# A long-convolution block and a linear-attention block in one kernel: the first inverse DFT stage in 32-row array tiles, with new channel groups, shift weights spread by a matmul, a shorter index computation and a new order

## The chip, the cores and the metric

The kernel runs on one core of a Trainium2 chip. The metric is the device time in microseconds of one execution; the median of three runs is given. Profile times are counted from the first instruction of the program. Engines are named as in the profile: PE is TensorE's matmuls and PEld its weight loads, DVE is VectorE, ACT is ScalarE, POOL is GpSimd, and SP is SyncE, which issues all DMAs here.

## The reference

Two independent blocks on 2048 positions and 576 channels, in bf16, side by side in the output:

```python
# A: gated long convolution
k_shift = sum over t < 4 of shift_k[:, t] * (k delayed by t)
kv = k_shift * v
y = irfft(rfft(pad(kv, 2S)) * rfft(pad(ssm_k, 2S)))[:S]     # along the 2048 positions, per channel
a = q * (y + kv * ssm_D)
# B: linear attention, 32 heads of 18 channels
q, k, v = split(x @ wqkv);  phi(t) = where(t > 0, t + 1, exp(t)) + 1e-6
kv = phi(k)^T v ;  z = sum phi(k)                            # per head
b = (phi(q) kv / (phi(q) z + 1e-6)) @ wo
out = concat(a, b)
```

## The kernel before

Block A does the transforms as matmuls. A position is split as 16 a + b with 128 values of a and 16 of b. The 576 channels come in five chunks (`ACH`, ci = 0 to 4), four of 128 and one of 64. For every chunk the same stages run on `ssm_k` (key h) and on the product kv (key u):

- `hl`, `hT`: load the rows of ssm_k and transpose them on PE (16 transposes of 128 x 128).
- `cv` (four stages): k_shift times v, on DVE or POOL, in place over v.
- `h1`, `u1` (`s1`, L460): first stage, for each b a matmul of 128 rows with the table `G[ri]` (ri = 0 cosine, 1 sine); 8 values of b make a unit, copied out of PSUM to `Ch` or `Cu`.
- `ht`, `ut` (`tr`, L467): a DMA transpose SBUF to SBUF, half a chunk (hf = 0, 1) at a time.
- `h2`, `u2` (`s2`, L483): second stage, the 16-point part: eight matmuls of 64 rows by 32 columns with 512 moving columns, into `T` (for h) or `SU` (for u).
- `pX`, `pT`: the products of the two spectra, on DVE.
- `i1` (L507): first inverse stage, below.
- `i2` (L520, L521): second inverse stage, with `F[ri]`, the transposed tables (`FT`), then the multiplication by q on DVE; `st` stores.

A half of `T` or `X` holds, on the 128 partitions, four bands of 32: (r, j), with r the pair and j the member. Before, an i1 unit treats one z of one half. For each of four column groups it accumulates four matmuls of 64 rows (a pair of bands) and 128 moving columns of the 16-point table `K.W`, for both pairs r; the two pairs lie in different row tiles of the array and write different PSUM banks. One unit is 32 matmuls, one PSUM tile and one copy to `V`. `K.W` has 128 columns, three quarters of which a mask makes zero in every row.

Block B has units `k` (L397) and `q` (L406), the projections from `xT` with phi on ACT (exp) and DVE (L389, L390); `G` (L570), phi(k)^T x; `kv`, `M`, `den`, `bc`; and `o` (L644), the output projection, whose result ACT copies to `ob` and SP stores. `xd` loads x transposed by DMA, `xl` loads it plain, `lw` loads the weights of q (0) and k (1).

All PSUM tiles come from one pool of four buffers of two banks each. The inputs k, v and q come in three channel groups (`GRP`) of 256, 256 and 64 channels (`kl`, `vl`, `ql`); v and q of the first two groups share two buffers.

Before the stages, a setup makes the tables. DVE multiplies two iotas into the index `mp` (L138), takes it modulo 8192 (L139), makes `ident` (L62), and makes `mc`, the index moved by three quarters of a turn, in two steps (L142, L143). ACT takes the sine of `mp` (`sin.1`) and of `mc` (`sin.0`), L212. Of the 16-point tables, index and mask are made on POOL and DVE (`iw`, `wk`, `iv`, `sw`, `W`). `wu.40` is 40 matmuls on zeros. The shift weights are loaded with a DMA that writes them to all 128 partitions (`ls`, `Wall`), and ACT reorders them to `Wj`.

What runs when is written by hand in `ORDER`: a list of units such as `i1.0.0.1.A` (chunk 0, half 0, z 1, copied by ACT). Each unit issues its instructions on every engine's queue in that order, and each engine works through its queue in order. A letter A, D or P at the end chooses the engine.

Of the kernel before, what the change touches and what calls it, by code (L numbers as in the profile page):

```python
# [26 lines left out]
ACH = [(0, 128), (128, 128), (256, 128), (384, 128), (512, 64)]  # L27
# [3 lines left out]
wm io wu.0 ix.0 sin.1 id ix.1 hl.0 iw wk wu.40 sin.0 hT.0.D FT.1.D h1.0.0.0.A h1.0.1.0.A FT.0.D h1.0.1.1.A  # L31
h1.0.0.1.A iv sw W lw.0 xd.2 q.2.0 hc lw.1 k.8 q.2.2 q.2.1 ls Wj hl.1 hT.1.D k.9 k.11 k.10 h1.1.1.0.D xd.0 k.3
kl.0 cv.0.0.D one h1.1.0.0.A k.1 ht.0.0 h2.0.0.0.A h2.0.0.1.A eps cv.0.1.DD cv.0.2.DD q.0.1 h1.1.1.1.A q.0.0
h1.1.0.1.A xd.3 q.3.0 q.0.2 vl.0 cv.0.3.PDD k.2 cv.1.0.P k.0 ht.0.1 h2.0.1.1.A q.3.1 k.12 u1.0.1.1.A k.15
h2.0.1.0.D ht.1.1 h2.1.1.0.A k.13 u1.0.0.1.A hl.2 hT.2.D u1.0.0.0.A cv.1.1.PD k.14 xd.1 u1.0.1.0.A xl.2
cv.1.2.DD cv.1.3.DPP ht.1.0 xl.1 h2.1.1.1.A q.1.1 h2.1.0.1.A h2.1.0.0.A q.1.0 q.1.2 h1.2.1.0.A ut.0.1 k.7
u2.0.1.0.D u2.0.1.1.A k.6 h1.2.0.1.A k.4 ut.0.0 u2.0.0.1.D u2.0.0.0.A k.5 pX.0.0 pT.0.0 u1.1.1.0.A u1.1.1.1.A
q.3.2 u1.1.0.1.A xl.0 xl.3 kl.1 pX.0.1 pT.0.1 u1.1.0.0.A es G.0 vl.1 h1.2.0.0.A h1.2.1.1.A cv.2.0.D cv.2.1.DD
cv.2.2.DD G.2 ut.1.0 G.4 u2.1.0.1.D u2.1.0.0.A ut.1.1 i1.0.0.1.A hl.3 i1.0.0.0.A i1.0.1.1.A i1.0.1.0.A
cv.2.3.DDD ql.0 cv.3.0.D cv.3.1.DD u2.1.1.1.A ht.2.0 u2.1.1.0.A pX.1.1 pT.1.1 hT.3.A G.1 lwv pX.1.0 pT.1.0  # L40
h2.2.0.1.A ht.2.1 G.3 cv.3.2.DD u1.2.0.0.A i2.0.0 kl.2 u1.2.1.1.A u1.2.1.0.A kv u1.2.0.1.A i2.0.1 h2.2.0.0.A
h2.2.1.0.A den h2.2.1.1.A i1.1.1.0.A lwo M.0 i1.1.0.1.A i1.1.0.0.A i1.1.1.1.D ut.2.0 u2.2.0.0.A M.2 ut.2.1
bc.3.0 u2.2.0.1.A bc.0.1 h1.3.0.1.A bc.4.0 h1.3.0.0.A bc.0.0 h1.3.1.1.A vl.2 h1.3.1.0.A hl.4 ht.3.0 i2.1.1 M.1
# [68 lines left out]
def _small(tc, cpool, slot, K):  # L112
# [9 lines left out]
    nc.vector.memset(K.negpi[:], -math.pi)  # L122
    K.warm = cpool.tile([128, 1], FP32, name="warm")
# [7 lines left out]
def _dft_index(tc, slot, K, part):  # L131

    nc = tc.nc
    if part == 0:
        kap = K.sm[:, 128:256].unsqueeze(1).to_broadcast([128, 16, 128])
        sv = K.sm[:, 256:272].unsqueeze(2).to_broadcast([128, 16, 128])
        K.mp = slot([128, 16, 128], I32, "mp")
        nc.vector.tensor_tensor(out=K.mp[:], in0=kap, in1=sv, op=ALU.mult)  # L138
        nc.vector.tensor_single_scalar(out=K.mp[:], in_=K.mp[:], scalar=8191, op=ALU.bitwise_and)  # L139
    else:  # L140
        K.mc = slot([128, 2, 16, 128], I16, "mc")
        nc.vector.tensor_single_scalar(out=K.mc[:, 0], in_=K.mp[:], scalar=6144, op=ALU.add)  # L142
        nc.vector.tensor_single_scalar(out=K.mc[:, 1], in_=K.mc[:, 0], scalar=8191, op=ALU.bitwise_and)  # L143


def _w16_index(tc, K):
# [21 lines left out]
    iota(sm[:, 384:448], [[1, 16], [0, 4]])  # L168
    for c, shift, mask in ((6, 1, 127), (8, 0, 1)):
# [23 lines left out]
def _w16_mask(tc, K):  # L193
# [5 lines left out]
    K.wz = K.sm[:, 1152:1536]  # L199
    nc.gpsimd.memset(K.wz, 1.0 / S)  # L200
    for p in (0, 64):
        m = K.wz[p:p + 64].rearrange("p (y z) -> p y z", z=4)
        nc.gpsimd.affine_select(out=m, in_=m, compare_op=ALU.is_ge, fill=0.0, base=0, pattern=[[0, 96], [-16, 4]],
                                channel_multiplier=1)
        nc.gpsimd.affine_select(out=m, in_=m, compare_op=ALU.is_ge, fill=0.0, base=15, pattern=[[0, 96], [16, 4]],
                                channel_multiplier=-1)


def _sine(tc, cpool, K, ri):
    K.G[ri] = cpool.tile([128, 16, 128], BF, name="G%d" % ri)  # L210
    src = K.mp[:] if ri else K.mc[:, 1]
    tc.nc.scalar.activation(out=K.G[ri][:], in_=src, func=ACT.Sin, scale=TWO_PI / 8192, bias=K.negpi[:])  # L212
# [512 lines left out]
```

## Time and profile before

| | |
|---|---|
| median of 3 runs | 171.53 us (171.33 to 173.3) |
| profiled execution, device time | 171.81 us |
| its span, first to last instruction | 170.0 us |
| PE busy | 159.0 us (94%) |
| DVE, ACT, POOL busy | 139.7, 122.8, 70.9 us (82%, 72%, 42%) |
| DMA, mean over the span | 192 GB/s, 32.58 MB |

The profile's page gives the busy time of each engine and then the span in 40 slices of 4.25 us, where a digit is the busy share in tenths. The groups collect equal instructions: count, busy time, mean duration, then the engine's idle time before them and what ended it. Matmuls overlap, so their mean duration is a latency and not a pitch. The chain of waits is followed back from the last instruction: each piece gives start, duration, engine, output and line, and how many instructions it merges. The timeline gives start, time to the end of the last one, engine, line, operation and shapes.

### The profile page before, as it was taken

Reading aid. Unit: us, or ns where it says so; the run is one execution under the profiler, and the core shown is the slowest. Engines: PE = TensorE matmul, PEld = TensorE weight load, DVE = VectorE, ACT = ScalarE, POOL = GpSimd, SP = SyncE. Lnnn points to the kernel's source line nnn. Section 1 sums busy time; section 2 is a strip of 40 time slices with the busy share of each in tenths; the row PEclk is TensorE's granted clock in tenths of the full one; section 3 lists DMA queues with packets and bytes.
Section 4 is the critical chain, followed back from the end, with each engine's and each line's share of the span. In section 5 each row is a group of like instructions: output and inputs, shape, how many; then the busy total and the mean of one; then the engine's idle time right before and its main releaser. Section 6 shows DMA issues by size and latency. Waiting matters only on the chain.

```text
span 170.0 us, 4984 instructions
## 1 busy us (share of the span) xinstructions
PE 159.0 (94%) x2176; PEld 106.9 (63%) x2176; DVE 139.7 (82%) x159; ACT 122.8 (72%) x142; POOL 70.9 (42%) x76
## 2 busy tenths in 40 slices
PE   4779999999999799999999999999999999999990
PEld 4768566665575456565685586857856765677750
DVE  7995589998989867999599887997999777999530
ACT  3458987977788899923597477989897778784431
POOL 7998982027693397000000049999900400000000
PEclk9999999999999999999999999999999999999997
DMA  5999699799989999999998655980959957988685
GB/s 147 273 268 250 119 267 136 137 272 225 145 183 217 263 178 318 290 213 219 306 214 196 106 150 40 182 159 18 146 126 276 202 128 69 237 180 258 191 244 117
DMA packets 81704, 32.58 MB, mean 192 GB/s; under 512 B 57432, under 2 KB 80978, under 8 KB 81682
## 3 DMA queue, kind: packets, MB, share of 16 engines
q1 hardware_dynamic: 81682, 32.26, 91.0%
q8 instruction: 17, 0.28, 0.7%
q14 instruction: 5, 0.04, 0.1%
HBM read 15.48 MB, written 4.72 MB: 119 GB/s over the span
## 4 chain that ended last, share of the span: by engine, by line
PE 77%; DMA 11%; DVE 6%; ACT 3%; issue 0%; ACTq 0%
PE q_ps L406 12%; PE g_ps L570 12%; PE k_ps L397 11%; PE o_ps L644 10%; PE s_ps L460 8%; PE i_ps L507 8%; DMA Ctu<-Cu 7%; PE s_ps L483 5%; DMA Cth<-Ch 4%; PE hT_ps L443 2%; PE i_ps L520 2%; PE i_ps L521 2%; PE bc_ps L635 1%; PE kv_ps L583 1%; DVE mp L138 1%; DVE mp L139 1%
## 5 line engine op out<-in xcount | busy, mean ns | idle before, releaser
L429 POOL TENSOR_TENSOR at<-k,Wj 128x2048 bf16<-128x2048 bf16 (+1 forms) x5 | 16.4, 3289 | 36.3 <-DVE at L430 36.2
L406 PE MATMUL q_ps<-xT,wqk 128*126 128x512 bf16 (+1 forms) x100 | 23.3, 381 | 0.0
L644 PE MATMUL o_ps<-wo_M,pqT 126*128 126x512 bf16 (+3 forms) x160 | 21.9, 286 | 0.0
L397 PE MATMUL k_ps<-wqk,xT 128*128 128x512 bf16 (+1 forms) x160 | 21.8, 286 | 0.0
L460 PEld LDWEIGHTS <-G 128*128 128x128 bf16 x320 | 17.6, 98 | 5.2 <-issue 2.1
L570 PE MATMUL g_ps<-pk,x_sb 128*128 128x512 bf16 (+3 forms) x160 | 20.4, 286 | 0.0
L277 ACT ACTIVATE Cu<-s_ps 128x1024 bf16<-128x1024 f32 (+1 forms) x18 | 16.6, 951 | 2.8 <-PE s_ps L460 2.4
L397 PEld LDWEIGHTS <-xT 128*128 128x128 bf16 x160 | 11.4, 98 | 11.1 <-issue 1.1
L644 PEld LDWEIGHTS <-pqT 126*128 126x128 bf16 (+1 forms) x160 | 11.2, 97 | 10.7 <-issue 0.8
L406 PEld LDWEIGHTS <-wqk 128*126 128x126 bf16 (+1 forms) x100 | 12.5, 131 | 8.2 <-issue 1.2
L277 ACT ACTIVATE Ch<-s_ps 128x1024 bf16<-128x1024 f32 (+1 forms) x18 | 16.3, 952 | 1.4 <-PE s_ps L460 0.8
L507 PE MATMUL i_ps<-W,T 64*128 64x128 bf16 x288 | 16.6, 216 | 0.4 <-DVE pqT L638 0.4
L649 ACT ACTIVATE ob<-o_ps 128x576 bf16<-128x576 f32 x16 | 10.4, 653 | 8.9 <-PE o_ps L644 8.7
L570 PEld LDWEIGHTS <-x_sb 128*128 128x128 bf16 (+1 forms) x160 | 10.8, 101 | 9.5 <-issue 0.2
L507 PE MATMUL i_ps<-W,X 64*128 64x128 bf16 x288 | 16.5, 216 | 0.0
L277 ACT ACTIVATE T<-s_ps 128x1024 bf16<-128x1024 f32 x16 | 15.8, 1021 | 0.6 <-PE s_ps L483 0.6
L277 ACT ACTIVATE V<-i_ps 128x1024 bf16<-128x1024 f32 x14 | 13.6, 1027 | 2.8 <-PE i_ps L507 2.1
L390 DVE SCALAR_TENSOR_TENSOR pqT<-pqT,q_ps 126x1024 bf16<-126x1024 bf16 (+1 forms) x12 | 12.2, 1037 | 3.8 <-ACT pqT L389 3.8
L522 DVE TENSOR_TENSOR q<-i_ps,q 128x1024 bf16<-128x1024 f32 (+1 forms) x10 | 11.2, 1116 | 4.6 <-PE i_ps L521 4.6
L389 ACT ACTIVATE pqT<-q_ps,neg 126x1024 bf16<-126x1024 f32 (+1 forms) x12 | 11.6, 968 | 4.3 <-PE q_ps L406 4.3
L430 POOL TENSOR_TENSOR at<-at 128x2048 bf16<-128x2048 bf16 (+1 forms) x4 | 12.4, 3094 | 5.4 <-DVE at L429 5.2
L433 POOL TENSOR_TENSOR v<-at,v 128x2048 bf16<-128x2048 bf16 (+1 forms) x3 | 10.3, 3419 | 9.8 <-DVE at L430 9.6
(120 smaller groups left out, 335.4 us busy)
## 6 DMA issues: line engine op xcount, KB each, us to landing
x_sb<-in_B_x_dram SPq DMA_DIRECT2D x4, 576.0 KB
out_dram<-ob SPq DMA_DIRECT2D x16, 144.0 KB, 4.0
h_sb<-in_A_ssm_k_dram SPq DMA_DIRECT2D x4, 512.0 KB
k<-in_A_k_dram SPq DMA_DIRECT2D x2, 1024.0 KB, 9.1
v<-in_A_v_dram SPq DMA_DIRECT2D x2, 1024.0 KB, 6.6
q<-in_A_q_dram SPq DMA_DIRECT2D x2, 1024.0 KB
out_dram<-q SPq DMA_DIRECT2D x2, 1024.0 KB
wqk<-in_B_wqkv_dram SPq DMA_DIRECT2D x2, 576.0 KB
```

The source lines that it names most:

```text
L277: nc.scalar.activation(out=out, in_=in_, func=ACT.Copy)
L389: nc.scalar.activation(out=out_ap, in_=ps_ap, func=ACT.Exp, bias=K.neg1[0:n, :])
L390: nc.vector.scalar_tensor_tensor(out=out_ap, in0=out_ap, scalar=1.0, in1=ps_ap, op0=ALU.min, op1=ALU.max)
L397: nc.tensor.matmul(ps[:, n0:n1], lhsT=xT[r // 4][:, t, rr * 128:(rr + 1) * 128], rhs=wqk[:, t, D + n0:D + n1], start=(t == 0), stop=(t == 4))
L406: nc.tensor.matmul(ps[0:hn, j, :], lhsT=wqk[:, t, h0:h0 + hn], rhs=xT[g][:, t, :], start=(t == 0), stop=(t == 4))
L429: on[0].tensor_tensor(out=t_, in0=kk[:, 3 - stage:19 - stage], in1=wb(stage), op=ALU.mult)
L430: on[1].tensor_tensor(out=a_, in0=a_, in1=t_, op=ALU.add)
L460: nc.tensor.matmul(ps[:, bi, 0:dc], lhsT=K.G[ri][:, b, :], rhs=xf(b), start=True, stop=True)
L507: nc.tensor.matmul(ps[:, r, g, :], lhsT=s[key, hf][64 * r:64 * r + 64, z, x, 128 * g:128 * g + 128], rhs=K.W[64 * r:64 * r + 64, m, :], st ...
L522: nc.vector.tensor_tensor(out=qs, in0=ps[:, :, 0:dc], in1=qs, op=ALU.mult)
L570: nc.tensor.matmul(ps[0:fn, n0:n1], lhsT=x_sb[:, r, f0:f0 + fn], rhs=pk[:, r, n0:n1], start=(r == 0), stop=(r == 15))
L644: nc.tensor.matmul(ps[:, n0:n1], lhsT=pqT[0:hn, c, r * 128:(r + 1) * 128], rhs=B['M'][0:hn, c, n0:n1], start=(c == 0), stop=(c == 4))
```

## The change

- The first inverse stage treats a whole half per unit, in bands of 32 rows: 128 matmuls of 32 rows and 64 moving columns, with the four bands (r, j) next to each other in program order, each in its own row tile of the array and its own PSUM bank. A unit holds two PSUM tiles and makes two copies. `K.W` shrinks to 64 columns, half of them zero in every row; its mask is made with one comparison on DVE instead of four POOL instructions; the factor 1/S moves from it to the copies of `FT`.
- So that the bands come out in that arrangement, `s1` reads its moving operand in a new channel order (runs of 8 channels), `s2` reads `Ct` in a contiguous order, and `i1` copies to `V` in runs of two.
- k, v, q come in two groups of 320 and 256 channels; the chunk of 64 channels is now the third of five. Each group of v and q has a buffer of its own (v's, then q's). `st` stores in three parts, the second group in two halves.
- The shift weights are loaded to one partition and spread over 128 by a matmul with a row of ones (`Wj.0`, `Wj.1`, `Wj.2`: 512 + 512, 512 + 512 and 256 columns), and copied by ACT to `Wj`.
- The index is reduced with a pair of shifts to the range -4096 to 4095, and `mc` is its absolute value (one instruction); the cosine is taken with a bias of half pi.
- `ORDER` is another one throughout. On DVE the two memsets of `wqk` (`wm`) stand behind the `FT` copies, and the memset of `ones1` behind the setup's index operations.

Two functions that transpose x on PE are defined and used by no unit of the order (left out below).

```diff
-ACH = [(0, 128), (128, 128), (256, 128), (384, 128), (512, 64)]
+ACH = [(0, 128), (128, 128), (256, 64), (320, 128), (448, 128)]
 ORDER = """
-wm io wu.0 ix.0 sin.1 id ix.1 hl.0 iw wk wu.40 sin.0 hT.0.D FT.1.D h1.0.0.0.A h1.0.1.0.A FT.0.D h1.0.1.1.A
-h1.0.0.1.A iv sw W lw.0 xd.2 q.2.0 hc lw.1 k.8 q.2.2 q.2.1 ls Wj hl.1 hT.1.D k.9 k.11 k.10 h1.1.1.0.D xd.0 k.3
...
+io hl.0 wk hl.1 wu.0 wu.40 ix.0 id sin.1 ix.1 iw ls Wj.2.A sin.0 lw.1 hT.0.D Wj.0.A Wj.1.A FT.1.D FT.0.D wm
+h1.0.1.1.A h1.0.0.0.A h1.0.0.1.D iv h1.0.1.0.A hT.1.D xd.1 sw k.5 one W k.4 k.6 lw.0 q.1.1 q.1.2 q.1.0 hc xd.3
...
+u1.3.1.1.A u1.3.1.0.D M.1 den h2.3.0.1.A ht.3.1 cv.4.1.PP cv.4.2.PP h2.3.0.0.A i1.2.0.AA hT.4.D M.2 h2.3.1.1.A
+i2.2.1 h2.3.1.0.A i2.2.0 h1.4.0.1.A bc.2.1 ut.3.0 M.0 h1.4.0.0.A bc.2.0 u2.3.0.1.A bc.3.1 ut.3.1 h1.4.1.1.A
+bc.4.1 pX.1.1 h1.4.1.0.A pT.1.1 M.4 u2.3.0.0.A ht.4.0 i1.1.0.AA bc.1.1 u2.3.1.1.A bc.0.1 M.3 bc.0.0 u2.3.1.0.A
+ht.4.1 i1.1.1.AA bc.3.0 cv.4.3.PPD o.8 pX.3.1 h2.4.0.1.A h2.4.0.0.A bc.4.0 o.15 u1.4.0.1.A bc.1.0 u1.4.1.1.A
...
+o.5 u2.4.1.0.A u2.4.1.1.D pX.4.1 pT.4.1 ql.1 o.7 o.0 u2.4.0.0.A i1.3.0.DA o.2 o.1 u2.4.0.1.D pX.4.0 pT.4.0 st.0
+i1.4.1.AD o.4 o.10 i1.4.0.AD i2.3.0 o.6 i2.4.0 st.1 i2.4.1 i2.3.1 o.14 st.2 o.3 o.12 o.11
 """
...
 def _dft_index(tc, slot, K, part):
-        nc.vector.tensor_single_scalar(out=K.mp[:], in_=K.mp[:], scalar=8191, op=ALU.bitwise_and)
+        nc.vector.tensor_scalar(out=K.mp[:], in0=K.mp[:], scalar1=19, scalar2=19, op0=ALU.logical_shift_left,
+                                op1=ALU.arith_shift_right)
     else:
-        K.mc = slot([128, 2, 16, 128], I16, "mc")
-        nc.vector.tensor_single_scalar(out=K.mc[:, 0], in_=K.mp[:], scalar=6144, op=ALU.add)
-        nc.vector.tensor_single_scalar(out=K.mc[:, 1], in_=K.mc[:, 0], scalar=8191, op=ALU.bitwise_and)
+        K.mc = slot([128, 16, 128], I16, "mc")
+        nc.vector.scalar_tensor_tensor(out=K.mc[:], in0=K.mp[:], scalar=-1.0, in1=K.mp[:], op0=ALU.mult, op1=ALU.max)
...
 def _w16(tc, cpool, K):
-    K.W = cpool.tile([128, 3, 128], BF, name="W16")
-    nc.vector.tensor_tensor(out=K.W[:].rearrange("p m n -> p (m n)"), in0=K.wz, in1=ws[:, 64:448], op=ALU.mult)
+    K.W = cpool.tile([128, 3, 64], BF, name="W16")
+    nc.vector.scalar_tensor_tensor(out=K.W[:].rearrange("p m n -> p (m n)"), in0=K.wz, scalar=K.tb, in1=ws[:, 64:256],
+                                   op0=ALU.is_equal, op1=ALU.mult)
...
-    Wall = slotv([128, D, 4], BF, "Wall")
+    Wrow = slotv([1, D, 4], BF, "Wrow", 1)
+    ones1 = lpool.tile([1, 128], BF, name="ones1")
...
     def load_shift():
-        nc.sync.dma_start(out=Wall[:].rearrange("p d j -> p (d j)"),
-                            in_=A_shift_k.rearrange("d j -> (d j)").partition_broadcast(128))
-    def shift_w():
-        nc.scalar.activation(out=Wj[:], in_=Wall[:].rearrange("p d j -> p j d"), func=ACT.Copy)
+        nc.vector.memset(ones1[:], 1.0)
+        nc.sync.dma_start(out=Wrow[:].rearrange("p d j -> p (d j)"), in_=A_shift_k.rearrange("(o d) j -> o (d j)", o=1))
+    def shift_w(i, eng='A'):
+        d0, dn = ((0, 256), (256, 256), (512, 64))[i]
+        ps = psum.tile([128, 256, 4], FP32, name="w_ps", tag="big")
+        for d in range(0, dn, 128):
+            n = min(128, dn - d)
+            nc.tensor.matmul(ps[:, d:d + n, :], lhsT=ones1[:], rhs=Wrow[:, d0 + d:d0 + d + n, :], start=True, stop=True)
+        evict(Wj[:, :, d0:d0 + dn], ps[:, 0:dn, :].rearrange("p d j -> p j d"), eng)
...
-    GRP = ((0, 256), (256, 256), (512, 64))
+    GRP = ((0, 320), (320, 256))
...
     def s1(ci, xf, key, bg, ri, eng='A'):
-            nc.tensor.matmul(ps[:, bi, 0:dc], lhsT=K.G[ri][:, b, :], rhs=xf(b), start=True, stop=True)
+            nc.tensor.matmul(ps[:, bi, 0:dc].rearrange("p (z h y) -> p z h y", z=2, y=8), lhsT=K.G[ri][:, b, :],
+                             rhs=xf(b).rearrange("p (h z y) -> p z h y", z=2, y=8), start=True, stop=True)
...
-    def i1(ci, hf, z, eng='A'):
+    def i1(ci, hf, eng='AA'):
...
-        ps = psum.tile([128, 2, 4, 128], FP32, name="i1_ps", tag="big")
-        for g in range(4):
-            for n, (key, x, m) in enumerate((('T', 0, 0), ('T', 1, 1), ('X', 0, 2), ('X', 1, 2))):
-                for r in range(2):
-                    nc.tensor.matmul(ps[:, r, g, :], lhsT=s[key, hf][64 * r:64 * r + 64, z, x, 128 * g:128 * g + 128],
-                                     rhs=K.W[64 * r:64 * r + 64, m, :], start=(n == 0), stop=(n == 3))
-        d = dc // 2 * z + 32 * hf
-        evict(V[:, :, d:d + 32].rearrange("p j (g t) -> p g j t", t=4),
-              ps[:].rearrange("p r g (j t) -> p (r g) j t", t=4), eng)
+        ps = [psum.tile([128, 2, 2, 4, 64], FP32, name="i1_ps", tag="big") for _ in range(2)]
+        for z in range(2):
+            for g in range(4):
+                for n, (key, x, m) in enumerate((('T', 0, 0), ('T', 1, 1), ('X', 0, 2), ('X', 1, 2))):
+                    for r in range(2):
+                        for j in range(2):
+                            q = 32 * (2 * r + j)
+                            nc.tensor.matmul(ps[r][:, j, z, g, :], lhsT=s[key, hf][q:q + 32, z, x, 128 * g:128 * g + 128],
+                                             rhs=K.W[q:q + 32, m, :], start=(n == 0), stop=(n == 3))
+        for r in range(2):
+            d = 64 * hf + 32 * r
+            evict(V[:, :, d:d + 32].rearrange("p j (c t) -> p c j t", t=2),
+                  ps[r][:].rearrange("p j z g (n t) -> p (j z g) n t", t=2), eng[r])
...
 def f_T(ri, eng='D'):
-        evict(K.F[ri][:], ps[:], eng)
+            nc.vector.tensor_single_scalar(out=K.F[ri][:], in_=ps[:], scalar=1.0 / S, op=ALU.mult)
```

More of the change, by code (lines that the diff above doesn't have):

```diff
@@ L39 @@
[L39 to L43, printed above, removed]
@@ L122, in _small @@
     nc.vector.memset(K.negpi[:], -math.pi)
+    K.halfpi = cpool.tile([128, 1], FP32, name="halfpi")
+    nc.vector.memset(K.halfpi[:], math.pi / 2)
     K.warm = cpool.tile([128, 1], FP32, name="warm")
@@ L167, in _w16_index @@
     iota(sm[:, 32:64], [[0, 2], [1, 16]])
-    iota(sm[:, 384:448], [[1, 16], [0, 4]])
-    for c, shift, mask in ((6, 1, 127), (8, 0, 1)):
+    iota(sm[:, 384:416], [[1, 16], [0, 2]])
+    for c, shift, mask in ((6, 1, 127), (8, 0, 1), (10, 0, 16)):
         n = sm[:, c:c + 1].bitcast(I32)
```

87 lines of the change are left out of this document (47 added, 40 removed).

## The prediction, made before the changed kernel was run

> **What bounds the kernel now.** I read the page first: busy shares, then the slices.
>
> ```profile
> span 170.0 us, 4984 instructions
> PE 159.0 (94%) x2176; PEld 106.9 (63%) x2176; DVE 139.7 (82%) x159; ACT 122.8 (72%) x142; POOL 70.9 (42%) x76
> PE   4779999999999799999999999999999999999990
> ```
>
> TensorE (PE) has work in every slice but the first three, one of 7 and the last. So a microsecond of PE work taken out of the middle is worth about a microsecond, as long as DVE, at 82%, doesn't become the bound. Second, the groups with shapes kept apart, and the chain of waits in order of time:
>
> ```profile
> L507 PE MATMUL i_ps<-W,T 64*128 64x128 bf16 x288 | 16.6, 216 | 0.4 <-DVE pqT L638 0.4
> L397 PE MATMUL k_ps<-wqk,xT 128*128 128x64 bf16 x80 | 4.9, 193 | 0.0
> ```
>
> ```profile
> 18.82 3.24 PE q_ps L406 x15
> ...
> 61.87 0.56 PE s_ps L483 x16
> 62.43 1.33 PE k_ps L397 x10
> 63.76 0.45 PE s_ps L460 x8
> 64.20 1.23 PE k_ps L397 x10
> ...
> 105.38 0.11 PE den_ps L614 x19
> ...
> 148.01 3.72 PE i_ps L507 x128
> ```
>
> The means in the groups are latencies of overlapping matmuls; the chain gives the pitch. 15 matmuls of 512 columns take 3.24 us, 216 ns each. A k block is five of those and five of 64 columns: 1.23 - 5 x 0.216 = 0.15 us, so a matmul of 64 columns with its own load of 128 weights takes 30 ns. Four i1 units (L507, 128 matmuls of 64 rows, two row tiles at once) take 3.72 us: 0.93 us a unit, 58 ns a pair. The k block right after an s2 stretch, whose matmuls sit in 64 x 32 tiles, takes 1.33 instead of 1.23 us: changing the array's tiling costs 0.10 us. And 19 matmuls of one column in four column tiles take 0.11 us, 5.8 ns each: where four tiles lie side by side, load and matmul can issue that fast.
>
> Third, the start, in PE's timeline and in the chain:
>
> ```profile
> 2.40 4.45 PE L73 MATMUL warm_ps<-sm 128*128 128x128 bf16 x40 [2.40 <-DVE sm L75]
> 7.84 1.86 PE L443 MATMUL hT_ps<-ident,h_sb 128*128 128x128 bf16 x16 [1.00 <-DVE ident L62]
> 9.50 1.90 PE L529 MATMUL ft_ps<-ident,G 128*128 128x128 bf16 x16
> 12.56 1.07 PE L460 MATMUL s_ps<-hT,G 128*128 128x128 bf16 x16 [1.16 <-ACT G L212]
> 13.46 1.06 PE L529 MATMUL ft_ps<-ident,G 128*128 128x128 bf16 x16
> ```
>
> ```profile
> 2.34 2.16 DVE mp L138
> 4.52 2.13 DVE mp L139
> 6.65 1.14 DVE ident L62
> 7.79 1.08 DVE mc L142
> 8.89 1.59 DVE mc L143
> ```
>
> Until about 12 us a DVE chain sets the time, and PE runs at half rate: the first 16 transposes take 9.50 - 7.84 = 1.66 us (104 ns each), the FT of 13.46 only 0.90 (56 ns).
>
> **First inverse stage.** Before: 18 units x 0.93 = 16.7 us. After: nine units of 128 matmuls, each 32 rows by 64 columns, in four row tiles, so 32 groups of four. No row shows four row tiles with 64 columns. Lower bound of a group: 27 ns, half of a pair's 58 less some fixed part; the nearest rows are the 64-column matmul with its load (30 ns) and the four column tiles (4 x 5.8 = 23 ns), so I take 30. Upper bound: 4 x 29 = 116 ns, if row tiles do not overlap beyond the rate at which the pairs issue today. At 30 ns a unit is 0.96 us, nine are 8.6: **-8.1 us**, all on PE in the second half, where PE sets the time.
>
> **Changes of tiling.** Counting in the two orders the places where an i1, s2 or den unit stands beside another kind gives 49 before and 62 after, since each i1 now stands alone: 13 x 0.10 = **+1.2 us**.
>
> **The start.** The two memsets of wqk (0.99 to 2.19 on DVE) go behind the FTs, so mp starts at about 1.3, when POOL's iotas (0.91 and 1.11, up to 0.24 us long) are done. Then 2.25 (2.27 to 4.52 today) + 2.13 (shift pair, priced as L139) + 1.14 (ident) = 6.8. One step makes mc out of two int32 operands: between 1.59 (L143) and 2.25 (L138), nearer the second: 9.05. That is 1.4 us earlier than today. But the first Wj matmul has been put ahead of hT on PE, and it waits for the ones1 memset, which stands on DVE behind mc and six small index operations (four take 0.4 us today): 9.7. Behind that matmul on PE stands hT, which could have run at 6.9; behind its copy on ACT stands the cosine (sin.0), which then ends at 12.8 instead of 12.5. So PE: hT at 9.95 instead of 7.84, at half rate to 11.6; four Wj matmuls of 512 columns at half rate, 4 x 0.43, to 13.3; then FT.1. Today the rate doubled after 3.4 to 4.7 us of steady work (7.84 to between 11.20 and 12.56); from 9.75 that is 13.1 to 14.5. With 14.5, FT.1 ends at 14.8, FT.0 at 15.7, the four first s1 at 17.5. Today these are done at 15.27: **+2.2 us**. With 13.1 it is +1.4; if the rate rises only behind FT.0 (the 40 warm-ups ran 4.45 us without it), +3.1.
>
> [...]
>
> **Loads.** hl.1 goes ahead of the first x (0.52 MB more before it; at the 1.0 MB in 6.6 us of a v load, +3.4 us). Today's x is in by 14.6, as its POOL memset runs there without a wait; the first k unit now asks at about 18.5, so hidden, with half a microsecond left. The 0.59 MB broadcast of the shift weights goes, which pays for k's first group being 320 channels wide; the first conv today runs at 30.0 without a wait. ql.1 (1.05 MB) now stands in the tail, behind three output stores on SP. From there to i2.3.0, which needs it, lie six o units (7.4), three i1 (2.9), two s2 (0.5) and an i2 half (0.9), 11.7 us, against 6.6 to 9.1 to land: 0, and if that cover were gone, its lateness moves the end one to one.
>
> **Costed at nothing.** s1 reads its moving operand in runs of 8 elements; no row shows that. Nearest is the strided stationary operand of hT, 62 against 56 ns: 0 to 6 ns x 320 = 0 to +2.0 us; I take 0, as a run of 8 lies nearer to contiguous than hT's single elements. A gain below today's 56 ns is excluded by the 128 columns. FT's copy now multiplies: 0 to +0.9 (L139 for the same size). V's copies write runs of 2 instead of 4: today runs of 4 cost 1027 against 1022 ns contiguous, so 0; the 18 copies stay 18. Conv on POOL grows by two full operations; POOL is at 42%.
>
> **Waits.** PE waits for buffers and transposes after the start add up to some 3.4 us today. An i1 now needs two of the four PSUM tiles at once, and its two copies (ACT, 0.94 each) last longer than its matmuls. I added PE, ACT and DVE by stretches of 15 us of PE work, each unit at its row: behind the start, DVE or ACT exceed PE by 1.7 us before and 4.2 after, worst around M.1 to o.8 (PE 17.3, DVE 19.6, ACT 19.9). So -3.4 (all waits gone) to +2.5; I take 0, because units may slide across a stretch's edge and the order is a new one throughout.
>
> **Sum.** 170.0 - 8.1 + 1.2 + 2.2 + 0 = 165.3 us of span. The profiled execution took 171.81, 1.8 outside its span: 167.1. The median of the runs, 171.53, lies 0.3 below that execution: **166.8 us**.
>
> **Rivals.**
> *Waits take it back*: the two-tile i1 and a busier DVE cost +2.5 to +4 in the middle: 169.3 to 170.8. For: DVE would be at about 137 of 165. Against: today's order holds PE waits to 3.4 us at 82%.
> *The row tiles issue one after the other*: in the first inverse stage each of 1152 matmuls takes the 29 ns that one of a pair takes today: 33.4 us, +16.7 instead of -8.1: 191.6 us, slower. Break-even is a group of four at 46 ns. For: no row has four row tiles, and a pair never runs under 58 ns. Against: the 5.8 ns of the four column tiles, and 58 ns is just the time of 128 columns.
> [...]
> *Only two of four run at once* (the change doesn't do what it says): 60 ns a group, 17.3 us, +0.6 instead of -8.1: 175.5.
> *Runs of 8 halve s1's rate*: 256 x 56 + 64 x 30 ns = +16.3: 183. Against: hT's far worse stride costs 10%.
>
> **How the numbers follow.** Forecast 0.61, its own range 163.4 (all waits gone) to 168.9 (start +3.1, runs +1.2). Waits take it back 0.21; only two at once 0.07; one after the other 0.06; halved s1 0.05. A difference of 2% (168.1 to 175.0) is about what a measurement of this kernel tells from no change. Faster: 0.57 of the forecast and 0.05 of the waits, 0.62; the rest of these two and half of "two at once" is within 2%, 0.22; slower 0.16. The range for 8 in 10 takes in forecast and waits: 162.5 (a bit below "all waits gone", for groups at 27 ns) to 172.5.
>
> **What would show it.** Right: 128 i1 matmuls in about 0.96 us; the first s1 ending near 17.5 with hT behind a Wj matmul; s1 still 0.45 us per 8; ACT and DVE waits of PE around M.1 to o.8. Wrong: an i1 unit over 1.5 us, s1 over 0.55 us per 8, i2.3.0 waiting for q, or PE gaps of over 6 us behind the start.

## The result, and the profile after

The changed kernel takes 194.91 us (median of 4 runs, 194.64 to 197.28) against 172.18 for the kernel before on the same chip: 1.135 times as long, 95% interval 1.123 to 1.146. The prediction was 166.8 us, in a range of 162.5 to 172.5, so it was wrong by 28 us and in its sign. Ratios in this document leave disturbed runs out; a median does not, so where the two differ the ratio is the figure to read.

The page of the changed kernel, the same rows as those shown of before, with the granted clock:

```profile
span 192.6 us, 6147 instructions
PE 164.9 (86%) x2757; PEld 105.6 (55%) x2757; DVE 147.6 (77%) x161; ACT 124.9 (65%) x146; POOL 71.1 (37%) x70
PE   7399999999999999859999914869779949987692
PEclk9859999999999999966999985999999996999999
```

Every engine's share fell: nothing became a bound by its amount of work. PE now has holes in the middle (the 1 near 113 us, the 4 behind it) and in the last third, and behind them the granted clock drops to 0.50. Measuring how far each matmul's start lies behind the median pace of its kind (line, tile and shape), PE loses 22 to 27 us more behind 20 us than before; the figure depends on the excess from which one counts. That is most of the 27 us between the predicted span (165.3) and the measured one.

Two things that the sum counted on did come. The start, in the chain of waits (start, duration, what):

```profile
3.62 1.23 DVE mp L141
4.85 0.23 DVE ident L61
...
8.21 0.38 PE w_ps L365
8.59 1.86 PE hT_ps L464 x16
...
15.52 1.92 PE s_ps L481 x32
```

The first four s1 are done at 17.44; 17.5 was predicted. And the row tiles run four at once, as PE's timeline shows of one i1 unit (8 matmuls to a row, start and latency):

```profile
154.96 0.25 PE L532 MATMUL i_ps<-W,T 32*128 32x64 bf16 x8
155.03 0.20 PE L532 MATMUL i_ps<-W,X 32*128 32x64 bf16 x2
157.89 0.23 PE L532 MATMUL i_ps<-W,X 32*128 32x64 bf16 x6 [2.66 <-issue]
158.06 2.14 PE L673 MATMUL o_ps<-wo_M,pqT 126*128 126x512 bf16 x8
```

In the undisturbed stretches of these units eight matmuls start every 62 to 65 ns, 31 to 33 ns to a group of four; 30 was predicted. But two matmuls into the second row's eight, PE stands still for 2.86 us. "issue" means that the profile shows nothing that it waited for: no operand, no buffer, no semaphore. The o unit behind it runs at half rate for a while (eight matmuls in 2.14 us, with a granted clock of 0.50 from 158.44 us; at the end of the kernel forty take 4.95). The second kind of hole is in the timelines of DVE and of POOL, around 110 us:

```profile
106.15 1.22 DVE L279 CAST Ch<-s_ps 128x1024 bf16<-128x1024 f32 x1
107.28 4.70 DVE L515 TENSOR_TENSOR X<-SU,T 128x2048 bf16<-128x2048 bf16 x1
112.02 4.95 DVE L517 TENSOR_TENSOR T<-SU,T 128x2048 bf16<-128x2048 bf16 x1
```

```profile
106.84 4.06 POOL L451 TENSOR_TENSOR at<-at 128x2048 bf16<-128x2048 bf16 x1
110.98 4.91 POOL L450 TENSOR_TENSOR at<-k,Wj 128x2048 bf16<-128x2048 bf16 x1
```

In the kernel before, all eighteen of these products take 1.2 us, and POOL's operations on as many elements 4.07 (groups of the kernel before):

```profile
L429 POOL TENSOR_TENSOR at<-k,Wj 128x2048 bf16<-128x2048 bf16 x3 | 12.2, 4066 | 36.2 <-DVE at L430 36.2
...
L495 DVE TENSOR_TENSOR T<-SU,T 128x2048 bf16<-128x2048 bf16 x9 | 10.9, 1222 | 0.2
L493 DVE TENSOR_TENSOR X<-SU,T 128x2048 bf16<-128x2048 bf16 x9 | 10.9, 1217 | 0.5 <-ACT T L277 0.4
```

X lasts until 111.98, 1.08 us longer than the POOL operation that began before it (106.84 + 4.06 = 110.90); T until 116.97, 1.08 longer than the next (115.89). It looks as if each waited for POOL to end and then took its own microsecond, and POOL's second operation, 4.91 instead of 4.06, for X in its turn. What reads PSUM beside POOL here, the Ch copy of 106.15 and the multiplication by q of 105.01, takes 1.22 and 1.23 us. PE's list of waits (total, times, longest) names the victim, s1 behind a q step that stood behind T on DVE. The wait for `wv_GT` comes from a third such product (77.93 to 82.90 us, 4.97 long), beside POOL's operation of 76.81 to 81.81:

```profile
PE s_ps L481 <- DVE q L548: 6.5, 1, 6.5
PE i_ps L532 <- issue: 5.2, 4, 2.7
...
PE s_ps L481 <- ACT wv_GT L603: 2.6, 1, 2.6
```

So there were two suspects. **Theory L (lock)**: a DVE operation with both operands in SBUF and a POOL operation that reads SBUF hold each other up. **Theory F (fetch)**: a run of very short PE instructions outruns the fetching of instructions. F came from counting PE's instructions, weight loads included: the six unexplained gaps lie at PE's instructions 3009, 3777, 4289, 4801, 5057 and 5313, all of which leave 193 when divided by 256 (block crossings, below), and the DMA queue that the page calls "instruction" moves its 0.34 MB in 21 packets of 16 KB. PE has 5525 instructions in this trace, 21 times 256 and a rest; before there were 4362, 17 times 256 and a rest, and 17 packets. From these counts I took one packet for 256 instructions, an estimate. **Rival W**: PE waits because the new i1 unit holds two PSUM tiles until two copies are done.

### The profile page after: what moved, and what is told of

It reads as the page before. It is cut to its first block, busy times and chain, and to the rows that moved or that the text cites. A ratio compares the mean times of both kernels' runs of the same rounds, so it can differ in the third digit from the quotient of the medians.

```text
span 192.6 us, 6147 instructions
## 1 busy us (share of the span) xinstructions
PE 164.9 (86%) x2757; PEld 105.6 (55%) x2757; DVE 147.6 (77%) x161; ACT 124.9 (65%) x146; POOL 71.1 (37%) x70
## 4 chain that ended last, share of the span: by engine, by line
PE 65%; DVE 16%; issue 8%; ACT 6%; DMA 2%; SPq 1%; POOL 0%; DVEq 0%; POOLq 0%; ACTq 0%
PE q_ps L427 12%; PE k_ps L418 10%; PE o_ps L673 9%; PE g_ps L599 7%; PE s_ps L481 7%; PE s_ps L505 4%; PE i_ps L532 4%; DVE pqT L667 4%; DVE X L515 3%; PE hT_ps L464 3%; DMA Cth<-Ch 2%; ACT Ch L277 2%; PE i_ps L546 2%; DVE wo_M L650 2%; PE ft_ps L555 2%
## 5 line engine op out<-in xcount | busy, mean ns | idle before, releaser
L450 POOL TENSOR_TENSOR at<-k,Wj 128x2048 bf16<-128x2048 bf16 (+1 forms) x6 | 24.3, 4048 | 35.4 <-issue 19.7
L481 PEld LDWEIGHTS <-G 128*128 128x128 bf16 x320 | 18.9, 102 | 12.6 <-issue 11.1
L599 PE MATMUL g_ps<-pk,x_sb 128*128 128x65 bf16 (+3 forms) x160 | 22.7, 302 | 0.0
L481 PE MATMUL s_ps<-v,G 128*128 128x128 bf16 (+1 forms) x160 | 11.6, 232 | 9.4 <-DVE q L548 6.5
L277 ACT ACTIVATE T<-s_ps 128x1024 bf16<-128x1024 f32 x18 | 17.6, 1021 | 2.0 <-PE s_ps L505 2.0
L517 DVE TENSOR_TENSOR T<-SU,T 128x2048 bf16<-128x2048 bf16 x9 | 18.5, 2054 | 0.3
L277 ACT ACTIVATE Cu<-s_ps 128x1024 bf16<-128x1024 f32 (+1 forms) x15 | 13.7, 939 | 6.9 <-PE s_ps L481 6.7
L673 PEld LDWEIGHTS <-pqT 126*128 126x128 bf16 (+1 forms) x160 | 11.4, 101 | 12.0 <-issue 2.9
L427 PEld LDWEIGHTS <-wqk 128*126 128x126 bf16 (+1 forms) x100 | 12.3, 131 | 8.4 <-issue 1.7
L277 ACT ACTIVATE SU<-s_ps 128x1024 bf16<-128x1024 f32 x15 | 15.1, 1034 | 1.5 <-PE s_ps L505 1.5
L532 PE MATMUL i_ps<-W,X 32*128 32x64 bf16 x576 | 11.6, 191 | 5.2 <-issue 5.2
L451 POOL TENSOR_TENSOR at<-at 128x2048 bf16<-128x2048 bf16 (+1 forms) x4 | 15.2, 3793 | 0.3
L515 DVE TENSOR_TENSOR X<-SU,T 128x2048 bf16<-128x2048 bf16 x9 | 14.4, 1604 | 0.2
L411 DVE SCALAR_TENSOR_TENSOR pqT<-pqT,q_ps 126x1024 bf16<-126x1024 bf16 (+1 forms) x12 | 12.3, 1037 | 2.9 <-ACT pqT L410 2.8
```

Of the source, the lines that this page charges most:

```text
L277: nc.scalar.activation(out=out, in_=in_, func=ACT.Copy)
L411: nc.vector.scalar_tensor_tensor(out=out_ap, in0=out_ap, scalar=1.0, in1=ps_ap, op0=ALU.min, op1=ALU.max)
L427: nc.tensor.matmul(ps[0:hn, j, :], lhsT=wqk[:, t, h0:h0 + hn], rhs=xT[g][:, t, :], start=(t == 0), stop=(t == 4))
L450: on[0].tensor_tensor(out=t_, in0=kk[:, 3 - stage:19 - stage], in1=wb(stage), op=ALU.mult)
L451: on[1].tensor_tensor(out=a_, in0=a_, in1=t_, op=ALU.add)
L481: nc.tensor.matmul(ps[:, bi, 0:dc].rearrange("p (z h y) -> p z h y", z=2, y=8), lhsT=K.G[ri][:, b, :], rhs=xf(b).rearrange("p (h z y) -> p ...
```

## Experiments

### One suspect out of the changed kernel at a time

**e1: late convolutions on DVE.**

```
-cv.3.0.P ... cv.4.1.PP cv.4.2.PP ... cv.4.3.PPD
+cv.3.0.D ... cv.4.1.DD cv.4.2.DD ... cv.4.3.DDD
```

> The changed kernel with the seven convolution steps that it gives to POOL behind 70 us (cv.3.0, the first two of cv.4.1 and of cv.4.2, the first two of cv.4.3) on DVE instead; everything else as in the changed kernel. Theory L (a DVE product with both operands in SBUF and a POOL tensor_tensor hold each other up): the products of L515 and L517 take 1.2 us everywhere and none near 5 us; the PE gaps of 2.7 us near 81 and 6.6 us near 112 go, and G behind the first gap runs at the full clock (4.0 us instead of 6.1). DVE gets some 7 x 1.2 = 8.5 us more work. About 183 us (180 to 187) instead of 194.9. Rival W (PE waits because the new i1 unit holds two PSUM tiles until two copies are done): the products are a side effect, PE's gaps stay, and DVE, busy for 77% of the span, gets longer: 195 to 203 us.

Measured: median 190.47, ratio to before 1.093 (1.079 to 1.107), some 7 us less than the changed kernel by the ratios. All products take 1.2 us again; the gaps of 2.7 and 6.6 us are gone, and DVE's busy time even falls, from 147.6 to 143.7 us, with seven more operations on it. L holds, W's 195 to 203 does not. But it is less than the 8 to 15 us expected. In the profiled execution, at 191.01 us one of the longer ones, the gaps at block crossings are 11.4 us in seven places against 9.2 in six, and PE waits at three new ones (1.31, 1.25 and 1.59 us, for a transpose, for hT's copy and for a convolution step on DVE); that these account for the rest is not shown.

**e3: tiles undone.**

```
-i1.0.0.AA
+i1.0.0.0.A i1.0.0.1.A      (two half units of 32 matmuls, 64 rows by 128 columns, as before; s1, s2 and the table too)
```

> The changed kernel with its matmul tiles undone: the first inverse stage in tiles of 64 rows with 64 matmuls to a half unit, as before, s1 and s2 and the table of the first inverse stage as before; order, POOL's convolutions, the groups of channels and the shift weights as in the changed kernel. By the sum of the prediction undoing it costs 8.1 - 1.2 = 6.9 us. Theory F: it also takes away the fetch gaps (some 9 us, with what the clock loses behind them): 189 to 196 us. Without F (only the lock between DVE and POOL and waits): 200 to 204 us. The products near 5 us stay under both.

Measured: 188.74, ratio 1.094 (1.085 to 1.102). The part of the change that was to save 6.9 us costs 6 to 7, although e3 starts 1.7 us later (its first four s1 are done at 19.13 us, with the old mask on POOL again). With it go all the gaps at block crossings (none over 0.5 us); the products of 4.97, 4.10 and 4.95 us stay. That is just below F's 189 to 196 and far from the 200 to 204 without F.

**e2: the units cut in two.**

One of the five units:

```
-... i1.1.1.AA ... o.8
+... ia.1.1 ... o.8 ib.1.1.AA
```

> The changed kernel with five of its nine i1 units (1.1, 3.1, 3.0, 4.1, 4.0) cut in two halves of 64 matmuls, with a unit of the output product (32 to 40 matmuls of longer duration) between the halves; the convolutions stay where they are. Theory F (a run of more than 256 short PE instructions outruns the fetch of instructions): the gaps of 0.95 to 2.85 us that lie at the crossing of a block of 256 instructions behind 127 us, together some 9 us, shrink by half or more: 187 to 191 us. Rival W (PSUM tiles and their copies set the gaps): the two tiles of a unit are held longer than before, so the waits stay or grow: 194 to 199 us.

Measured: 192.89, ratio 1.116 (1.105 to 1.126) against 1.135, about 3 us. The gaps at crossings fell from 9.2 to 5.8 us (1.37 of these the profile puts down to ACT's copy of V), short of "by half or more", and the time lies between the two expectations. It supports F weakly.

**e5: both out, e10: the short start as well, e12: two convolution steps later.** e5 joins the edits of e1 and e3; e10 takes e7's start (below); e12 moves two units in e10's order:

```
-ht.3.1 cv.4.1.DD cv.4.2.DD h2.3.0.0.A ... ut.3.0 M.0 h1.4.0.0.A bc.2.0
+ht.3.1 h2.3.0.0.A ... ut.3.0 M.0 cv.4.1.DD h1.4.0.0.A bc.2.0 cv.4.2.DD
```

> The changed kernel with both suspects taken out: its late convolution steps on DVE instead of POOL (as in e1) and its matmul tiles of 64 rows as before (as in e3). If the lock and the fetch are separate causes that add up, taking out both gives the sum of the two gains, 194.9 - 4 to 7 - 6 = 182 to 185 us, with no product of DVE near 5 us and no PE gap at a block crossing; what is then left above the 172 us of before comes from the start (2.2 us by the prediction, more here, since the mask of before is built on POOL beside DVE's index steps), the order and the tail. If they overlap (one gap merely taking the place of another): 186 us or more.

> The kernel of e5 (convolutions on DVE, tiles undone) with the start of e7: the short index and mask steps, nothing ahead of the first s1, the three units of shift weights by PE behind the first four s1. What is left of the changed kernel is the two groups of channels, the shift weights by PE and the searched order. If e5's distance to before is made of the start (first four s1 done at 19.1 us instead of 15.3) and of single late spots behind it, the start's 4 to 6 us come off: 180 to 182 us. If the work behind is bound by DVE anyway (79% busy, and the wait of 4.2 us near 120 us for a convolution step on DVE), it gains under 2 us: 184 to 186 us.

> The kernel of e10 (convolutions on DVE, tiles undone, short start; 183.1 us) with cv.4.1 and cv.4.2 moved from behind ht.3.1 to behind M.0 and bc.2.0. In e10 these four DVE steps of 1.15 to 1.24 us stand on DVE's queue between the reciprocal of den and the copy of hT.4, and PE waits 4.25 us near 116 us for that copy. If this spot is what is left of the distance: the wait goes, the output units start 3 to 4 us earlier than 136 us, and the time is 178 to 180.5 us. If the searched order is late in many places by itself (den 4 us later than before, the first bc 10 us later), the steps are only waited for elsewhere: 182 to 184 us.

Measured: e5 185.75, ratio 1.073 (1.067 to 1.080); e10 183.1, 1.065 (1.059 to 1.072); e12 182.36, 1.046 (1.038 to 1.054). So the gains of e1 (4.2 points) and e3 (4.1) overlap, 6.2 together; the start brings another 0.8 points, between the two expectations. In e12 the wait of 4.25 us for hT's copy went, and one of 2.86 us of a bc unit came, for ACT's copy of SU, which had waited for a product on DVE. By ratio that is a gain of some 3 us, but it rests on two runs (180.27 and 181.49; the others took 183.22 and 184.61), so I call it inconclusive. What is left, 5 to 6%, is partly waits: behind 20 us, those of e10 with 0.8 us and more between matmul starts add up to 8.5 us against 2.1 before, half of it the 4.26 us behind the convolution steps now on DVE, and behind that one the granted clock is 0.50 for 6.8 us. So taking the steps off POOL had a price on DVE. In e10 the first den unit starts at 108 us (104 before), the first bc at 121 (111), the first output unit at 136 (124). The order, the two groups of channels and the shift weights by PE were not taken apart further; which of them makes the outputs late stays open.

### Each suspect brought into the kernel before

**e8: POOL's idle time used.** The one edit:

```
-cv.3.0.D cv.3.1.DD
+cv.3.0.P cv.3.1.PP
```

> The kernel before with one edit of its order: the convolution steps cv.3.0 and cv.3.1 (three operations, near 88 to 92 us) go to POOL, which stands idle there from 67 to 100 us, and leave DVE. The products of chunk 1 (L493, L495), both operands in SBUF, then run beside POOL's operations. Theory L: they take up to 5 us each instead of 1.22, so do POOL's operations (4.06 to 5), DVE loses 3 to 4 us for each that it meets; PE waits for the first inverse stage: 176 to 182 us. Without a lock POOL's idle time is free, as the prediction took it: products 1.22 us, DVE 3.7 us lighter, and at most 3 us of waiting for cv.3.2's addition: 172 to 175 us.

Measured: 179.91, ratio 1.045 (1.037 to 1.052). Timelines of DVE and POOL:

```profile
89.59 3.12 DVE L493 TENSOR_TENSOR X<-SU,T 128x2048 bf16<-128x2048 bf16 x1 [2.16 <-ACT SU L277]
92.75 4.96 DVE L495 TENSOR_TENSOR T<-SU,T 128x2048 bf16<-128x2048 bf16 x1
97.64 4.05 DVE L448 TENSOR_TENSOR hT<-hT,Drow 1x128 bf16<-1x128 bf16 x1
```

```profile
87.57 4.06 POOL L427 TENSOR_TENSOR at<-k,Wj 128x2048 bf16<-128x2048 bf16 x1 [20.84 <-DMA Cth<-Ch]
91.59 5.04 POOL L429 TENSOR_TENSOR at<-k,Wj 128x2048 bf16<-128x2048 bf16 x1
96.71 4.91 POOL L430 TENSOR_TENSOR at<-at 128x2048 bf16<-128x2048 bf16 x1
```

One operation waits for the other as a whole: X, begun at 89.59, ends 1.08 us after the POOL operation of 87.57. DVE's third row is the clearest: a product of one row of 128 elements, 0.20 us before, takes 4.05 and ends 0.07 us after POOL's. Three operations taken off DVE made DVE's busy time longer (145.5 against 139.7 us), and PE has a gap of 5.9 us at 96.7, for a copy by ACT that waits for DVE behind that third row; behind the gap the granted clock is 0.50 for 6.8 us. Theory L is shown, in a kernel that has nothing else of the change.

**e4: the tiles alone.** s1, s2, i1 and the table from the changed kernel, each pair of half units merged where its second half stood.

> The kernel before with the matmul tiles of 32 rows alone (first inverse stage, s1, s2, the table), in the order of before, each pair of half units put together where the second half stood. By the prediction's sum 171.8 - 8.1 + 0.2 = 164 us where nothing else moves. Theory F (fetch): the units that follow one another closely lose 1 to 2.9 us each at the crossing of a block: 167 to 172 us. Rival W (two PSUM tiles to a unit): waits on copies around every unit, 170 to 176 us, with no gaps at the crossings of blocks. No product of DVE near 5 us under any of them.

Measured: 184.89, ratio 1.068 (1.058 to 1.078): 12 us slower than before where the sum says 8 faster, and worse than any of the expectations. No product is slow here. Seven gaps at block crossings make 11.5 us, the longest in the second of two adjacent units:

```profile
85.46 0.20 PE L508 MATMUL i_ps<-W,T 32*128 32x64 bf16 x2
89.22 0.29 PE L508 MATMUL i_ps<-W,T 32*128 32x64 bf16 x6 [3.56 <-issue]
```

The gaps alone aren't the 20 us between sum and measurement. Four spells at a granted clock of 0.50 make 20.5 us (86.84 to 93.67, 114.14 to 120.97, 141.45 to 144.87, 165.34 to 168.76), each with such gaps in it or just ahead of it. PE is busy for 16.0 us of them, so up to 8 more were lost there, an estimate.

**e6: more instructions, nothing else.** In the kernel before, each i1 matmul of 128 columns becomes two of 64:

```
 for g in range(4):
+    for c in (0, 64):
         for n, (key, x, m) in enumerate(...):
             for r in range(2):
-                nc.tensor.matmul(ps[:, r, g, :], ..., rhs=K.W[64 * r:64 * r + 64, m, :], ...)
+                nc.tensor.matmul(ps[:, r, g, c:c + 64], ..., rhs=K.W[64 * r:64 * r + 64, m, c:c + 64], ...)
```

> The kernel before, in its own order, with its own 64-row tiles, one PSUM tile and one copy to a half unit: only that each matmul of the first inverse stage (128 columns of the table) is cut in two of 64 columns, so that a half unit is 64 matmuls and 128 PE instructions with their weight loads instead of 64 in the same 0.95 us of PE work. Theory F (the fetch of instructions cannot follow so dense a run): PE gaps of 0.5 to 2.5 us appear at the crossings of blocks of 256 instructions inside or right behind these units, though nothing else was changed: 175 to 181 us instead of 172. Rival W (the gaps belong to the two PSUM tiles or the row tiles of the new unit): none appear, 171.5 to 173.5 us.

Measured: 183.18, ratio 1.056 (1.047 to 1.064), above even F's range. The tiles are those of before, with one PSUM tile and one copy to a half unit, and yet, in PE's timeline:

```profile
87.96 0.19 PE L508 MATMUL i_ps<-W,T 64*128 64x64 bf16 x2
90.67 0.20 PE L508 MATMUL i_ps<-W,T 64*128 64x64 bf16 x2 [2.51 <-issue]
```

The gaps of 1.82, 2.70, 1.28, 2.19 and 1.97 us lie at instructions that leave 182 to 184 when divided by 256, and 193 or 194 when the 9 to 11 matmul records that this trace lacks before them (fewer than its weight loads) are put back: the same places as in the changed kernel. W has nothing to say to this; F is shown. Over the changed kernel, e4 and e6 together, such a stall came only where the previous 256 PE instructions had taken under 4 us, though not at each such place (256 passed in 2.5 to 3.8 us without one at a few crossings); in the changed kernel and e4, these 256 and the stall together took 2.7 to 4.9 us. The kernel before is at the edge: its fastest 256 pass in 3.7 us without a stall, and in e7, below, 256 in 3.8 us meet one of 1.28. In the changed kernel the stall ended 2.3 to 2.5 us after the start of the fetch in the DMA records (155.42 to 157.89, 141.01 to 143.34, 168.73 to 171.13), of which the transfer took 0.9 to 1.1. Where 256 instructions took 5 us and more, no stall came: there the fetch was hidden. The 256 instructions of an i1 unit in 32-row tiles issue in 1.0 to 1.2 us, and PE then stood still for up to 3.75 us (e4).

### Can the tiles be had without the stalls?

**e11** takes e4 and puts a unit of long matmuls between the halves of each unit. **e13** and **e14** use e9 (below) and 32-row tiles for the last three units alone, each in two halves with output units around them; e14 builds the narrow table earlier and has an output unit behind the last half.

```
e11: -i1.0.0.AA i1.0.1.AA                     +ia.0.0 hl.3 G.1 ib.0.0.AA ia.0.1 G.3 ib.0.1.AA
e14: -i1.3.1.0.A i1.3.1.1.A i1.3.0.1.D st.0 i1.3.0.0.A   +ia.3.1 o.15 ib.3.1.AD ia.3.0 o.12 ib.3.0.AD
```

> The kernel of e4 (before with the tiles of 32 rows alone, 184.9 us) with each of its nine units cut in two halves of 64 matmuls (128 PE instructions) and a unit of longer matmuls (a G, an output, an M or a bc unit, 1 to 4 us of PE time with 10 to 64 instructions) put between the halves and mostly behind them. Theory F: fewer than 256 instructions now pass in any 2.5 us, and most of the 11.5 us of gaps at the crossings of blocks go: 172 to 177 us. Where the row tiles or the held PSUM tiles themselves were the cause, the time stays at 182 to 187 us. If all gaps went and nothing else was late, the sum of the prediction would hold: 164 to 166 us.

> The kernel of e9 (170.6 us) with the tiles of 32 rows for the last three units of the first inverse stage alone (chunks 3 and 4), where output units of long matmuls are at hand: each unit in two halves of 64 matmuls with an output unit or four s2 and other work between, s1 and s2 of these two chunks in the matching arrangement. By the prediction's price three units save 3 x (1.86 - 0.96) = 2.7 us less 0.3 for the extra changes of tiling: 168 to 168.5 us if no gap at a block crossing is left. Theory F with the dilution only half enough (1 us left per unit, as behind single units of the changed kernel): 170 to 172 us. If the tiles lose here as well: above 172 us.

> The kernel of e13 with two of its own late spots mended: the narrow table is built in place of the wide one as soon as chunk 2 is through (in e13 its step on DVE waited for POOL's last convolution step, 3.2 us of PE time, and PE ran at half rate behind), and an output unit stands behind the last half of each unit, so that the copies of V do not hold the second stage. What is left between it and e9 is the row tiles of three units, with long matmuls around them. By the prediction's price: 168 to 168.5 us. With about 1 us of fetch left per unit: 170 to 172 us. Above 172 us: the row tiles lose here as well.

Measured: e11 191.94, ratio 1.111 (1.104 to 1.118), a miss: the gaps at crossings shrank from 11.5 to some 3.0 us (1.04 and 1.92), but the G units now delayed everything behind them, and PE waits for copies by ACT and DVE at some twenty places. The edit asked two questions at once. e13 177.19, 1.023 (1.017 to 1.029), clouded by my own table: PE waited 2.8 us for it and then ran at half rate (ten matmuls of an output unit in 2.58 us, 1.40 elsewhere). e14 173.41, ratio 1.011 (1.008 to 1.014), with nothing else moved much: 2.1 points behind e9, where the price promised 2.4 us less. Small gaps of 0.2 to 1.0 us in and around its units add up to 4.0 us, against 1.1 in the same stretch of e9. So the tiles gained in no place where I tried them; whether a wider spacing could turn that was not tried.

### What can be kept

**e7: the start alone** (in the kernel before: shift pair, one-step cosine index, mask by comparison instead of four affine_selects on POOL, wqk's memsets behind FT). **e9** adds two moves, **e15** a third:

```
e7:  -wm io wu.0 ix.0 sin.1 id ix.1 hl.0 iw wk wu.40 sin.0 hT.0.D     +io hl.0 wu.0 ix.0 sin.1 id ix.1 wu.40 sin.0 hT.0.D iw wk
e9:  -h2.0.0.0.A h2.0.0.1.A eps cv.0.1.DD cv.0.2.DD q.0.1             +q.0.1 h2.0.0.0.A h2.0.0.1.A eps cv.0.1.DD cv.0.2.DD
     -i1.0.1.1.A i1.0.1.0.A cv.2.3.DDD ... hT.3.A G.1                 +cv.2.3.DDD ... i1.0.1.1.A hT.3.A i1.0.1.0.A G.1
e15: -ls Wj hl.1 hT.1.D ... xd.0                                      +hl.1 xd.0 ls hT.1.D Wj ...
```

> The kernel before with the part 'index in fewer steps' alone, and without the parts that put work ahead of the first stage: shift pair for the mask operation, one step for the cosine index, the block mask of the table as a comparison with two short iotas instead of a memset and four affine_selects on POOL, 1/S in the copy of F, and the two memsets of wqk moved behind the second copy of FT. By the rows: index product from 1.3 instead of 2.3 us, shift pair 1.23 instead of 2.13, identity 0.23 instead of 1.14 (no POOL work beside them), cosine index 2.2 instead of 2.7: G for the cosine ready near 9.3 instead of 12.5 us, first four s1 done near 12.3 to 13.5 instead of 15.3. If the loads for the first q and k products have landed by then, the end comes 1.5 to 3 us earlier: 169 to 171 us. Rival: the transposed load of x is not there earlier, and the gain is lost in a wait of q.2.0: 171.5 to 173 us.

> The kernel of e7 with two moves in its order: q.0.1 (2.2 us of PE work) ahead of h2.0.0, where PE waited 2.17 us for the transposed Ch, and the four adjacent half units of i1.0 taken apart into two and two with eight units between them, where a gap of 1.3 us lay at the crossing of a block. If both gaps are filled and nothing new is late, 1.5 to 3 us less than e7: 168 to 170 us, against 172 to 173 for the kernel before. If the waits only move (the transpose queue, or the products behind a later first inverse stage): 170.5 to 172 us.

> The kernel of e9 with the transposed load of the first group of x issued ahead of the load of the shift weights (590 KB at the core) instead of behind it. In e9 q.0.1 still waits 1.2 us near 30 us. If the load of the shift weights ahead of it is what makes it late, 169 to 170.3 us; if the transposes take their time whatever stands ahead, 170.4 to 171 us.

Measured: e7 171.24, ratio 0.987 (0.979 to 0.995); e9 170.60, 0.990 (0.986 to 0.994); e15 171.49, 0.997 (0.994 to 1.000). e9 is better than the kernel before, by 1.0% with a tight interval. That its two moves gain anything over e7 is not shown: the ratios overlap, and 170.60 lies in the expectation for waits that only move. Its page:

```profile
span 169.0 us, 4969 instructions
PE   7879999799899999999999999989999989999990
```

In e7 the first four s1 were done at 12.3 us, 3 us earlier than before, but PE then waited 2.17 us for the first transposed Ch; in e9 it waits some 1.2 us near 30 us. e15 took that for a wait for x, wrongly: the timeline puts it down to ACT's copy of T, and 171.49 lies above both its expectations. Bringing x sooner made PE wait 1.9 us at 23.9 (for a copy of pk on DVE) and gained nothing. Of 3 us gained at the start about 2 stay.

## Why the prediction was wrong, point by point

**First inverse stage, -8.1.** The pitch was right: 31 to 33 ns a group (30 taken), 1.0 to 1.2 us an undisturbed unit (0.96). Its rivals "one after the other" and "two at once" are out. What the term left out is the number of instructions: 1,152 matmuls instead of 576, each with its weight load, packed into the same microseconds. I asked how fast the array can take such matmuls and never how fast they can be delivered. e3 and e4 show that this turns the saving of 7 to 8 us into a loss of 6 to 12, and e6 that the instructions do it without the tiles.

**Changes of tiling, +1.2, and s1's runs of 8, 0.** The prices held: a change costs some 0.10 us still (a k block behind s2 takes 1.33 us, another 1.23), and s1 still takes 0.45 us per 8.

**The start, +2.2.** Right in sum (17.44 against 17.5), and in its cause (hT behind the first Wj matmul). Two of its rows were not: the shift pair took 1.23 instead of 2.13 us, the identity 0.23 instead of 1.14; what that gained was lost by the clock. The granted clock had risen to 1.00 at 4.84 us, fell to 0.50 at 8.26 behind PE's wait of 2.9 us for `ones1`, and rose at 15.1 only, behind nearly the whole of FT: after 6.9 us of steady work (8.21 to 15.08), where I had taken 3.4 to 4.7 from the trace of before. What sets this time was not shown. So that the sum came out to 0.1 us is partly luck: hT began 1.4 us sooner than in the sum, and more ran at half rate. The durations of before were those of operations beside POOL's affine_selects: e3, with the old mask on POOL, has 2.13 and 1.14 again.

**Loads, 0.** q was not what the tail waited for. Right.

**"Conv on POOL grows by two full operations; POOL is at 42%."** This is the first step that failed. It looked at the share and not at what runs beside: in the kernel before, every product of 2048 elements a partition on DVE with both operands in SBUF happens to lie clear of POOL's convolutions (none takes over 1.3 us), and in the changed kernel three begin beside one and take 4.97, 4.70 and 4.95 us (Ch and q, which read PSUM, 1.22 and 1.23). The trace of before has a small sign of it: its product of one row (`hT`, L448) at 51.86 us takes 0.43 us, 0.21 at 25.63, and ends 0.08 us after the POOL operation of 48.13 to 52.20 that it meets.

**"Waits": 0, at most +2.5.** This is the term that failed by size: PE's lost time grew by 22 to 27 us. Of that, 9.2 us are the stalls at block crossings and 9.1 the two waits behind slow products (2.6 and 6.5). The sum by stretches of 15 us compared totals of engines, and neither cause shows in a total: the lock made durations longer (4.95 instead of 1.22 us), and the stalls of the fetch stand in no engine's busy time. Behind such holes the clock was lost too: in 83.35 to 90.18, 114.07 to 120.90 and 158.44 to 161.86 us the granted clock was 0.50 in the profile's rows, and PE was busy for 12.6 of these 17.1 us, so that up to 6.3 us, an estimate, was lost there. Before has half rate only ahead of 12 us and at its end (granted 1.00 from 11.26 to 168.27 us). This accounts for the changed kernel's trace; it is not what taking the causes out gave back. Of 13.5 points, e5 gave back 6.2 and the short start 0.8; what the order, the channel groups and the shift weights by PE cost by themselves stays open.

**The rivals.** "Waits take it back" had the right mechanism's name and a tenth of its size. Two of the signs named for "wrong" came true: PE gaps of over 6 us behind the start, and i1 units of over 1.5 us (five of nine, 2.1 to 4.1 us). The waits of i1 for copies by ACT, in which the two-tile unit would show, come to 0.8 and 0.4 us. The chances of "within 2%" and "slower" add up to 0.235 and 0.145 from their own terms, not 0.22 and 0.16; nothing hangs on it.

## What to carry to other kernels

Before an operation is moved to an engine with time to spare, lay its span beside the operations of the engine that it leaves; a share of 42% says nothing on whether the two can run together. Price a finer tiling by its instructions as well as its array time: here, where a crossing stalled PE, 256 of its instructions and the stall took 2.7 to 4.9 us together (the changed kernel and e4), and an i1 unit, with matmuls 8 ns apart and their weight loads, asked for 256 in 1.0 to 1.2 us. And a gap that the profile puts down to "issue" is worth a count of instructions.

## What was not expected of the hardware

- An operation on one row of 128 elements took 4.05 instead of 0.20 us on DVE while POOL ran a tensor_tensor (e8).
- Four row tiles start matmuls 8 ns apart, weight loads included (31 ns for four), and 256 PE instructions then pass in 1.0 to 1.2 us.
- PE stalls of 0.56 to 3.75 us at instruction counts a multiple of 256 apart (the changed kernel, e4, e6), ending 2.2 to 3.0 us after the fetch's transfer began (transfer itself 0.9 to 1.8 us).
- The shift pair on int32 in SBUF takes 1.23 us without POOL's affine_selects beside it (the changed kernel) and 2.13 with them (e3); the identity comparison 0.23 and 1.14.
